# The end of a decode kernel: column tiles in two banks, projections ahead of V, and the last head woven into w4

## The chip, the cores and the metric

One NeuronCore of a Trainium2 chip runs the whole program. The time is that of one execution on the device, in microseconds (us), as the median over several runs. The profile is one execution taken by the hardware profiler; its times count from the start of its span. PE is TensorE, DVE is VectorE, ACT is ScalarE, POOL is GpSimd, and SP is SyncE, which here issues nearly all loads.

## The reference

Four tokens (B = 4, one position each, D = 576) go through a layer norm, and then through an attention block and an MLP block side by side, whose results are added:

```
xn = layernorm(x)
q  = xn @ wq                        # 32 heads of 128
k, v = the last 2048 positions of the caches, 16 heads, each used by 2 q heads
o  = softmax(q . k / sqrt(128)) @ v
A  = o @ wo                         # (4, 4096) @ (4096, 576)
h2 = gelu(layernorm(x1) @ w3) @ w4  # 576 -> 4608 -> 576
out = x + A + x1 + h2
```

With one position per token the shifts of the MLP's mixer move everything out of its single position, so that its first part adds zero and x1 is xn; w1 and w2 are not needed.

## The kernel before

The kernel is a stream of loads with work hung on it: wq, then 16 K tiles with w3 between the first of them, half of w4, 16 V tiles with eight tiles of wo between them, and the other half of w4. A K or V tile is one kv head of all four tokens, 2048 KB as 128 partitions x 64 chunks x 128. All of these loads are issued by SP, in the order of the program. SP waits with an issue until the buffer is free, and also until the load that stands eight issues back has landed; whatever is behind it on SP waits with it. The tiles of K, V, w3, w4 and the exponentials E share one pool of six buffers (`big`, NBUF, line 17), and wo has three of its own (line 87).

K is transposed on DVE (line 258), and scores of all heads add up in four banks S (line 267). `softmax` (from line 276) makes exponentials on ACT (line 283), normalizes them (lines 300 and 302), transposes the probabilities on PE (line 306) and puts them into PZ (lines 311 and 314).

The output of projection and MLP has 576 columns. PE computes them as two halves of DH = 288 columns, each on a 32-column tile of the array, with four rows (tokens) in use. So that four tiles work at the same time, the terms of the sums are shared between two pairs of tiles: in `acc_matmuls` (line 341) `half` picks the pair, and the result stands in partitions 64 x half + 32 x q. All four lie in one PSUM bank, ACC (line 182), which is zeroed once by a matmul (line 187). In its columns from 320 on, ACC also holds the MLP's first product. At the end the second pair is copied out (`second`, line 475) and added to the first (`fin`, line 481), and two small DMAs store the two halves of columns (line 483).

A row of w4 here is one of the 18 chunks into which each half of w4 is cut: 128 partitions x 576 elements, 147,456 bytes, two matmuls of 128x288. `load_w4(e, i0, n, cuts)` (line 420) takes one buffer for n rows of half e and fills it with one DMA for each number in `cuts`. `mlp_out` (line 431) does the matmuls of one piece, and its rows alternate between the two pairs of tiles, or use the first pair only where `last` is set. The first half is loaded whole ahead of V0 (line 452) and multiplied ahead of the softmax (line 457).

The V loop (line 461) stands under a manual schedule: PE's instructions keep the program's order there, while the other engines are ordered by the scheduler. For head v it issues V of head v + 4 and, for every second one, a tile of wo (lines 464 to 466). `v_compute(v)` (line 328) makes 16 matmuls into a bank O, four chunks at a time. `run_later` runs what the previous head left: for a pair of heads the projection (line 388, eight matmuls), and `select` of the head before (line 367). `head_out(v)` adds the four diagonal blocks of O into `osum` on DVE (lines 362 and 364). `select` lets PE sum and transpose osum (OT, line 370), DVE copy the result (`on`, line 372), PE spread it (line 375), and DVE write it to `onx` (line 383), the projection's stationary operand.

After the loop, half 1 of w4 is loaded in pieces of 9, 4, 2, 2 and 1 rows (line 470). PE multiplies the nine rows, runs the last head's select and the last projection, waits for `second`, and multiplies the last nine rows on the first pair alone (lines 471 to 477).

Of the kernel before, what the change touches and what calls it, by code (L numbers as in the profile page):

```python
# [12 lines left out]
F32 = mybir.dt.float32  # L13
# [7 lines left out]
def kernel(  # L21
# [18 lines left out]
    nc = tc.nc  # L40
    P = 128
    B, Sq, D = A_x.shape
    _, Hkv, Sk, Dh = A_k_cache.shape
    Hq = A_wq.shape[1] // Dh
    rep = Hq // Hkv
# [14 lines left out]
    NFH = NF // 2  # L60
    NQ = Hq * Dh
    DH = D // 2
# [26 lines left out]
    ps_s = ctx.enter_context(tc.tile_pool(name="ps_s", bufs=4, space=PSUM))  # L89
# [6 lines left out]
    def kv_load(win, h):  # L96
        t = big.tile([P, NCH, Dh], BF16, tag="big")
        nc.sync.dma_start(out=t[:].rearrange("p c d -> p (c d)"),
                          in_=win[:, h].rearrange("b (p c) d -> p b (c d)", p=G))
        return t  # L100
# [4 lines left out]
    XR = 4  # L105
# [24 lines left out]
    ident = const.tile([P, P], BF16)  # L130
# [27 lines left out]
    def transposed_pe(prep):  # L158
        src_bf, dup, T = prep
        tp = ps_tp.tile([P, KJ + 2, B], BF16, tag="tp")  # L160
        for j in range(KJ):
            nc.tensor.transpose(out=tp[:, j, :], in_=src_bf[:, j:KJ * P:KJ], identity=ident[0:B, 0:B])
        for e in range(2):
            nc.tensor.transpose(out=tp[:, KJ + e, :], in_=dup[:, e, :], identity=ident[0:B, 0:B])
        nc.vector.tensor_copy(out=T[:], in_=tp[:])

# [15 lines left out]
    ACC = ps_acc.tile([P, 512], F32)  # L182
    NR = 32 + B

    zeros = const.tile([P, 512], BF16)
    nc.vector.memset(zeros[:], 0.0)
    nc.tensor.matmul(out=ACC[:], lhsT=ident[:], rhs=zeros[:], start=True, stop=False, skip_group_check=True)
    GP0 = 320
    gp = ACC[:, GP0:GP0 + NF * B].rearrange("p (f b) -> p f b", b=B)
    gT = const.tile([P, NF, B], BF16)  # L190
# [35 lines left out]
    for y in range(NY):  # L226
        tq = ps_o.tile([P, 2 * HB, P], BF16, tag="O", name=f"tq{y}")
        for k in range(2):
            for m in range(HB):
                nc.tensor.transpose(out=tq[:, k * HB + m, :],  # L230
                                    in_=q_rows[:, k, m, y, :, :].rearrange("p g i -> p (g i)"), identity=ident[:])
# [18 lines left out]
    S = []  # L250
# [77 lines left out]
    def v_compute(h):  # L328
        bank = ps_o.tile([P, NI * Dh], F32, tag="O", name=f"O{h}")
        vn = V_tiles.pop(h)  # L330
        ns = NCH // (NI * NG)
        for s in range(ns):
            for j in range(NG):
                c0 = (s * NG + j) * NI
                nc.tensor.matmul(out=bank[G * j:G * j + G, :],  # L335
                                 lhsT=PZ[:, h, c0:c0 + NI, :].rearrange("p c m -> p (c m)"),
                                 rhs=vn[:, c0:c0 + NI, :].rearrange("p c d -> p (c d)"),
                                 start=(s == 0), stop=(s == ns - 1), skip_group_check=True)
        O_tiles[h] = bank

    def acc_matmuls(lhsT, rhs_cols, half):

        for q in range(2):
            o0 = 64 * half + 32 * q
            nc.tensor.matmul(out=ACC[o0:o0 + B, 0:DH], lhsT=lhsT, rhs=rhs_cols(q * DH, (q + 1) * DH),  # L345
                             start=False, stop=False, skip_group_check=True)

    wo_tiles = {}
# [2 lines left out]
    def load_wo(g2):  # L351
        wo_tiles[g2] = wop.tile([P, XR, D], BF16, tag="wo", name=f"wo{g2}")
        nc.sync.dma_start(out=wo_tiles[g2][:].rearrange("p x n -> p (x n)"), in_=wo_src[:, g2, :])

    later = []

    def head_out(h):


        bank = O_tiles.pop(h)  # L360
        osum = ktp.tile([P, Dh], F32, tag="kt", name=f"osum{h}")
        nc.vector.tensor_scalar_mul(out=osum[:], in0=bank[:, 0:Dh], scalar1=diag[:, 0:1])  # L362
        for i in range(1, NI):
            nc.vector.scalar_tensor_tensor(out=osum[:], in0=bank[:, i * Dh:(i + 1) * Dh], scalar=diag[:, i:i + 1],  # L364
                                           in1=osum[:], op0=ALU.mult, op1=ALU.add)

        def select():
            OT = ps_tp.tile([P, 64 + XR * rep * B], F32, tag="tp", name=f"OT{h}")
            T = OT[:, 64:64 + XR * rep * B].rearrange("p (x n) -> p x n", x=XR)
            nc.tensor.matmul(out=OT[:, 0:NB], lhsT=osum[:], rhs=sel[:], start=True, stop=True, skip_group_check=True)  # L370
            on = small.tile([P, rep, B], BF16, tag="on", name=f"on{h}")
            nc.vector.tensor_copy(out=on[:].rearrange("p r b -> p b r"),  # L372
                                  in_=OT[:, 0:NB].rearrange("p (b r) -> p b r", r=rep))
            for x in range(XR):
                nc.tensor.matmul(out=T[0:32, x, :], lhsT=ident[:, x:P:XR], rhs=on[:].rearrange("p r b -> p (r b)"),  # L375
                                 start=(x == 0), stop=(x == XR - 1), skip_group_check=True)
            g2, odd = divmod(h, 2)
            if not odd:
                onx_tiles[g2] = small.tile([P, XR, B], BF16, tag="onx", name=f"onx{g2}")
            onx = onx_tiles[g2]  # L380
            for r in range(rep):
                q = 32 * (2 * odd + r)
                nc.vector.tensor_copy(out=onx[q:q + 32, :, :], in_=T[0:32, :, r * B:(r + 1) * B])  # L383
            if odd:
                wt = wo_tiles.pop(g2)
                onx_tiles.pop(g2)

                def project():
                    for x in range(XR):
                        acc_matmuls(onx[:, x, :], lambda a, z, x=x: wt[:, x, a:z], x % 2)  # L390
                later.append(project)
        later.append(select)

    def run_later():
        fns = later[:]
        later.clear()
        for fn in fns:
            fn()

    def g_piece(t, j):  # L400
        for fc in range(NF):
# [18 lines left out]
    def load_w4(e, i0, n, cuts):  # L420
        t = big.tile([P, n, D], BF16, tag="big", name=f"w4_{e}_{i0}")
        parts = []
        a = 0
        for m in cuts:
            nc.sync.dma_start(out=t[:, a:a + m, :], in_=w4_src[e, :, i0 + a:i0 + a + m, :])
            parts.append((t[:, a:a + m, :], e, i0 + a, m))
            a += m
        assert a == n
        return parts

    def mlp_out(t, e, i0, n, last=False):
        for i in range(n):
            acc_matmuls(gT[:, e * NFH + i0 + i, :], lambda a, z, i=i: t[:, i, a:z], 0 if last else i % 2)


    for h in range(Hkv):
# [12 lines left out]


    NV0 = 4
    w4 = load_w4(0, 0, NFH, (NFH,))
    for v in range(NV0):
        V_tiles[v] = kv_load(v_win, v)
    for g2 in range(2):
        load_wo(g2)
    mlp_out(*w4[0])
    PZ = softmax()

    with tc.manual_schedule(engines={mybir.EngineType.PE}):  # L460
        for v in range(Hkv):
            n = v + NV0
            if n < Hkv:
                V_tiles[n] = kv_load(v_win, n)
                if n % 2 == 0:
                    load_wo(n // 2)
            v_compute(v)
            run_later()
            head_out(v)
        end = load_w4(1, 0, 9, (9,)) + load_w4(1, 9, 9, (4, 2, 2, 1))  # L470
        mlp_out(*end[0])
        while later:
            run_later()
        second = const.tile([P, DH], F32)
        nc.vector.tensor_copy(out=second[0:NR, :], in_=ACC[64:64 + NR, 0:DH])  # L475
        for part in end[1:]:
            mlp_out(*part, last=True)
    assert not K_tiles and not V_tiles and not wo_tiles

    fin = const.tile([P, DH], out.dtype)  # L480
# [33 lines left out]
```

## Time and profile before

| what | value |
|---|---|
| median of 3 runs | 216.41 us (216.26 to 216.51) |
| the profiled execution, its own time | 216.26 us |
| its span | 214.5 us |
| HBM read | 87.17 MB, 406 GB/s over the span |
| DVE busy | 130.2 us (61%) |
| PE busy | 112.2 us (52%), mean granted clock 0.676 |
| ACT busy | 21.0 us (10%) |

The span ends 1.76 us short of the time of that execution, since what lies around the span is not in it. A row of a group names the line, the engine, the operation, and then out<-in with the tiles' names; "x16" is a count. In the table of windows, each stretch has the busy time of each engine with the number of instructions, then the granted clock of TensorE (1.00 is full speed), the mean busy share of the 16 DMA engines and the rate at which they moved data. Ends of matmuls are modelled, so that a duration of one matmul is longer than the distance between two of them.

### The profile page before, as it was taken

To read this page: it belongs to the slowest core of one execution; us is meant where nothing else is said; L and a number is where in the kernel's file an instruction comes from. 1 tells how busy PE (TensorE), PEld (TensorE's weight loads), DVE (VectorE), ACT (ScalarE), POOL (GpSimd) and SP (SyncE) were. 2 spreads that over 40 slices of the span, in tenths; PEclk is the share of its full clock that TensorE was granted. 3 is DMA by queue.
4 is the path that set the end of the run, shared out by engine and by line. 5 is a ranking of instruction groups with operands and counts; after the bars stand their busy time and mean duration, and the time that the engine had idled before them with its cause. 6 is when DMAs were issued, how large, how long until landed. Compare 5 with 4: busy or idle time off the path is not lost.

```text
span 214.5 us, 4125 instructions
## 1 busy us (share of the span) xinstructions
PE 112.2 (52%) x1841; PEld 57.1 (27%) x1841; DVE 130.2 (61%) x223; ACT 21.0 (10%) x36; POOL 1.8 (1%) x8
## 2 busy tenths in 40 slices
PE   0383797774345544454442195735555554646374
PEld 0123484741111111111101162423232221313141
DVE  7949525369999999899675691862424142324241
ACT  0204100000000000000004896000000000000000
POOL 1110000000000000000000000000000000000000
PEclk9999995558579758665578569995555555555555
DMA  6999999999999999999999999999999999999940
GB/s 251 434 440 422 440 439 408 440 425 426 422 440 422 428 434 434 425 425 425 443 431 419 434 428 421 432 443 407 437 420 434 432 442 410 435 428 430 411 191 1
DMA packets 7529, 87.43 MB, mean 408 GB/s; under 512 B 844, under 2 KB 984, under 8 KB 2648
## 3 DMA queue, kind: packets, MB, share of 16 engines
q1 hardware_dynamic: 7496, 87.17, 95.8%
q8 instruction: 14, 0.23, 0.4%
q10 hardware_dynamic: 16, 0.01, 0.0%
q14 instruction: 3, 0.02, 0.0%
HBM read 87.17 MB, written 0.00 MB: 406 GB/s over the span
## 4 chain that ended last, share of the span: by engine, by line
DMA 66%; DVE 15%; PE 11%; ACT 5%; issue 2%; SPq 1%; DVEq 0%
DMA t<-in_A_v_cache_dram 38%; DMA t<-in_A_k_cache_dram 22%; DVE kt L258 10%; DMA wq<-in_A_wq_dram 6%; PE O L335 4%; PE ACC L345 3%; PE pt L306 2%; ACT E L283 2%; ACT PZ L311 1%; ACT pr L300 1%; DVE q_rows L224 1%; DVE pr L302 1%; PE qp L208 1%; PE OT L370 1%; DVE osum L362 0%
## 5 line engine op out<-in xcount | busy, mean ns | idle before, releaser
L258 DVE STREAM_TRANSPOSE kt<-t 128x2048 int32<-128x2048 int32 x32 | 72.0, 2290 | 15.4 <-DMA t<-in_A_k_cache_dram 15.4
L267 PE MATMUL S<-kt,qz 32*32 32x512 bf16 x1024 | 37.3, 625 | 40.2 <-DVE kt L258 37.8
L335 PE MATMUL O<-t,PZ 128*32 128x512 bf16 x256 | 27.9, 550 | 29.3 <-DMA t<-in_A_v_cache_dram 27.6
L362 DVE TENSOR_SCALAR osum<-O,diag 128x128 f32<-128x128 f32 x16 | 5.6, 350 | 39.8 <-PE O L335 39.8
L267 PEld LDWEIGHTS <-qz 32*32 32x32 bf16 x1024 | 10.6, 94 | 63.5 <-issue 59.9
L335 PEld LDWEIGHTS <-PZ 128*32 128x32 bf16 x256 | 9.2, 118 | 37.6 <-issue 33.9
L364 DVE SCALAR_TENSOR_TENSOR osum<-O,diag,osum 128x128 f32<-128x128 f32 x48 | 16.6, 348 | 1.0
L306 PE MATMUL pt<-ident,pr 128*128 128x128 bf16 x64 | 5.8, 265 | 9.2 <-DVE pr L302 8.2
L283 ACT ACTIVATE E<-S,nb 128x512 f32<-128x512 f32 x4 | 4.0, 1114 | 62.6 <-DMA t<-in_A_v_cache_dram 62.6
L370 PEld LDWEIGHTS OT<-sel,osum 128*128 128x128 f32 x32 | 7.2, 281 | 10.8 <-issue 5.2
L407 PEld LDWEIGHTS <-w 128*128 128x128 bf16 x144 | 9.1, 163 | 1.6 <-DMA w<-in_B_w_dram 0.8
L370 PE MATMUL OT<-sel,osum 128*128 128x8 f32 x32 | 8.6, 343 | 1.5 <-DVE osum L364 1.5
L407 PE MATMUL ACC<-ln2T,w 128*128 128x4 bf16 x144 | 9.3, 202 | 0.0
L300 ACT ACTIVATE pr<-E,rdm 128x512 bf16<-128x512 f32 x6 | 8.0, 1419 | 0.7 <-DVE rdm L289 0.7
L306 PEld LDWEIGHTS <-pr 128*128 128x128 bf16 x64 | 5.0, 121 | 10.5 <-ACT pr L300 10.3
L302 DVE TENSOR_SCALAR pr<-E,rdm 128x512 bf16<-128x512 f32 x10 | 6.4, 793 | 0.3 <-PE pt L306 0.2
L383 DVE CAST onx<-OT 32x16 bf16<-32x16 f32 x32 | 5.3, 165 | 2.0 <-PE OT L375 0.4
L375 PE MATMUL OT<-on,ident 128*32 128x8 bf16 x64 | 4.2, 171 | 4.1 <-DVE on L372 4.1
L345 PE MATMUL ACC<-wo,onx 128*4 128x288 bf16 x64 | 5.5, 424 | 0.4 <-DVE onx L383 0.4
L345 PE MATMUL ACC<-w,gT 128*4 128x288 bf16 x72 | 5.1, 366 | 0.9 <-DVE second L475 0.6
L375 PEld LDWEIGHTS <-ident 128*32 128x32 bf16 x64 | 4.5, 110 | 4.0 <-issue 3.6
L230 PE MATMUL tq<-ident,q_rows 128*128 128x128 bf16 x32 | 3.8, 312 | 2.7 <-ACT q_rows L222 2.7
(74 smaller groups left out, 62.9 us busy)
## 6 DMA issues: line engine op xcount, KB each, us to landing
t<-in_A_k_cache_dram SPq DMA_DIRECT2D x16, 2048.0 KB, 23.5
t<-in_A_v_cache_dram SPq DMA_DIRECT2D x16, 2048.0 KB, 21.8
w<-in_B_w_dram SPq DMA_DIRECT2D x2, 2304.0 KB, 24.9
wo<-in_A_wo_dram SPq DMA_DIRECT2D x8, 576.0 KB, 20.7
wq<-in_A_wq_dram SPq DMA_DIRECT2D x2, 2048.0 KB, 10.1
w<-in_B_w_dram SPq DMA_DIRECT2D x1, 2592.0 KB, 27.2
w<-in_B_w_dram SPq DMA_DIRECT2D x1, 1296.0 KB
w_t<-in_B_w_dram SPq DMA_DIRECT2D x1, 576.0 KB, 26.3
```

What stands on the lines that cost most here:

```text
L258: nc.vector.transpose(out=ap32(kt, e * G * 2, [[2 * G * 2, NCH // 2], [1, 2], [2, G]]), in_=ap32(kn, e * G, [[2 * 2 * G, NCH // 2], [2 * G ...
L267: nc.tensor.matmul(out=S[g][32 * b:32 * b + 32, :].rearrange("p (c k l) -> p c k l", k=GK, l=2), lhsT=qz[32 * g:32 * g + 32, b, h, y, :], ...
L283: nc.scalar.activation(out=E[:, :, g, :].rearrange("p (c l) k -> p c k l", l=2), in_=S[g][:].rearrange("p (c k l) -> p c k l", k=GK, l=2), ...
L300: nc.scalar.mul(out=dst, in_=src, mul=rdm[:, b:b + 1])
L302: nc.vector.tensor_scalar_mul(out=dst, in0=src, scalar1=rdm[:, b:b + 1])
L306: nc.tensor.transpose(out=tp[:, cc, :], in_=pr[:, half * HC + cc, :, :, :].rearrange("p g k b -> p (g k b)"), identity=ident[:])
L335: nc.tensor.matmul(out=bank[G * j:G * j + G, :], lhsT=PZ[:, h, c0:c0 + NI, :].rearrange("p c m -> p (c m)"), rhs=vn[:, c0:c0 + NI, :].rear ...
L345: nc.tensor.matmul(out=ACC[o0:o0 + B, 0:DH], lhsT=lhsT, rhs=rhs_cols(q * DH, (q + 1) * DH), start=False, stop=False, skip_group_check=True)
L364: nc.vector.scalar_tensor_tensor(out=osum[:], in0=bank[:, i * Dh:(i + 1) * Dh], scalar=diag[:, i:i + 1], in1=osum[:], op0=ALU.mult, op1=AL ...
L370: nc.tensor.matmul(out=OT[:, 0:NB], lhsT=osum[:], rhs=sel[:], start=True, stop=True, skip_group_check=True)
L375: nc.tensor.matmul(out=T[0:32, x, :], lhsT=ident[:, x:P:XR], rhs=on[:].rearrange("p r b -> p (r b)"), start=(x == 0), stop=(x == XR - 1), ...
L407: nc.tensor.matmul(out=gp[:, fc, :], lhsT=lhsT, rhs=rhs, start=False, stop=False, skip_group_check=True)
```

## The change

The second pair of column tiles gets a bank of its own: `ACC2`, a buffer of the pool `ps_s` (the one of S), zeroed by a matmul at the start of the manual schedule; `acc_matmuls` writes `ACCS[half]`. Until then only the first pair is used. The list `later` is split: projections run ahead of the next head's `v_compute`, selects stay behind it, and `select` is cut into `transpose_sum` (OT and `on`) and the rest. Of the first half of w4 only nine rows are loaded ahead of V0; the other nine come after V15, in front of half 1. So 27 rows are loaded at the end, in pieces of 9, 5, 4, 5, 3 and 1, and the steps of the last head stand between the pieces. `mlp_out`'s argument `last` is now called `one`.

```diff
@@ -185,6 +185,7 @@
     nc.tensor.matmul(out=ACC[:], lhsT=ident[:], rhs=zeros[:], start=True, stop=False, skip_group_check=True)
+    ACCS = [ACC]
@@ -340,9 +341,10 @@
     def acc_matmuls(lhsT, rhs_cols, half):
         for q in range(2):
             o0 = 64 * half + 32 * q
-            nc.tensor.matmul(out=ACC[o0:o0 + B, 0:DH], lhsT=lhsT, rhs=rhs_cols(q * DH, (q + 1) * DH),
+            nc.tensor.matmul(out=ACCS[half][o0:o0 + B, 0:DH], lhsT=lhsT, rhs=rhs_cols(q * DH, (q + 1) * DH),
                              start=False, stop=False, skip_group_check=True)
@@ -352,7 +354,7 @@
-    later = []
+    selects, projects = [], []
@@ -364,13 +366,16 @@
-        def select():
+        def transpose_sum():
             OT = ps_tp.tile([P, 64 + XR * rep * B], F32, tag="tp", name=f"OT{h}")
-            T = OT[:, 64:64 + XR * rep * B].rearrange("p (x n) -> p x n", x=XR)
             nc.tensor.matmul(out=OT[:, 0:NB], lhsT=osum[:], rhs=sel[:], start=True, stop=True, skip_group_check=True)
             on = small.tile([P, rep, B], BF16, tag="on", name=f"on{h}")
             nc.vector.tensor_copy(out=on[:].rearrange("p r b -> p b r"),
                                   in_=OT[:, 0:NB].rearrange("p (b r) -> p b r", r=rep))
+            return OT, on
+
+        def select(OT, on):
+            T = OT[:, 64:64 + XR * rep * B].rearrange("p (x n) -> p x n", x=XR)
@@ -388,14 +393,12 @@
-                later.append(project)
-        later.append(select)
-
-    def run_later():
-        fns = later[:]
-        later.clear()
-        for fn in fns:
-            fn()
+                projects.append(project)
+        selects.append((transpose_sum, select))
+
+    def run_projects():
+        while projects:
+            projects.pop(0)()
@@ -449,32 +452,43 @@
     NV0 = 4
-    w4 = load_w4(0, 0, NFH, (NFH,))
+    w4 = load_w4(0, 0, 9, (9,))
     for v in range(NV0):
         V_tiles[v] = kv_load(v_win, v)
     for g2 in range(2):
         load_wo(g2)
-    mlp_out(*w4[0])
+    mlp_out(*w4[0], one=True)
     PZ = softmax()
 
     with tc.manual_schedule(engines={mybir.EngineType.PE}):
+        ACC2 = ps_s.tile([P, 512], F32, tag="S", name="ACC2")
+        nc.tensor.matmul(out=ACC2[:], lhsT=ident[:], rhs=zeros[:], start=True, stop=False, skip_group_check=True)
+        ACCS.append(ACC2)
         for v in range(Hkv):
             n = v + NV0
             if n < Hkv:
                 V_tiles[n] = kv_load(v_win, n)
                 if n % 2 == 0:
                     load_wo(n // 2)
+            run_projects()
             v_compute(v)
-            run_later()
+            if selects:
+                tsum, select = selects.pop()
+                select(*tsum())
             head_out(v)
-        end = load_w4(1, 0, 9, (9,)) + load_w4(1, 9, 9, (4, 2, 2, 1))
+        end = load_w4(0, 9, 9, (9,)) + load_w4(1, 0, 9, (5, 4)) + load_w4(1, 9, 9, (5, 3, 1))
+        tsum, select = selects.pop()
         mlp_out(*end[0])
-        while later:
-            run_later()
+        last = tsum()
+        mlp_out(*end[1])
+        select(*last)
+        mlp_out(*end[2])
+        run_projects()
+        mlp_out(*end[3])
         second = const.tile([P, DH], F32)
-        nc.vector.tensor_copy(out=second[0:NR, :], in_=ACC[64:64 + NR, 0:DH])
-        for part in end[1:]:
-            mlp_out(*part, last=True)
+        nc.vector.tensor_copy(out=second[0:NR, :], in_=ACC2[64:64 + NR, 0:DH])
+        for part in end[4:]:
+            mlp_out(*part, one=True)
```

More of the change, by code (lines that the diff above doesn't have):

```diff
@@ L429, in load_w4, with mlp_out @@
         return parts
-    def mlp_out(t, e, i0, n, last=False):
+    def mlp_out(t, e, i0, n, one=False):
         for i in range(n):
-            acc_matmuls(gT[:, e * NFH + i0 + i, :], lambda a, z, i=i: t[:, i, a:z], 0 if last else i % 2)
+            acc_matmuls(gT[:, e * NFH + i0 + i, :], lambda a, z, i=i: t[:, i, a:z], 0 if one else i % 2)
     for h in range(Hkv):
```

## The prediction

> **What bounds the kernel now.** The page's slices over time come first.
>
> ```profile
> PE   0383797774345544454442195735555554646374
> ...
> PEclk9999995558579758665578569995555555555555
> DMA  6999999999999999999999999999999999999940
> GB/s 251 434 440 422 440 439 408 440 425 426 422 440 422 428 434 434 425 425 425 443 431 419 434 428 421 432 443 407 437 420 434 432 442 410 435 428 430 411 191 1
> ```
>
> A slice is 5.36 us. The DMA row is full from the second slice to the 38th (203.8 us), so up to there the time is bytes over rate and no engine matters. The changed kernel loads the same 87.17 MB. The last two slices are different: little or nothing is loaded, and 10.7 us pass. They are read from the chain that ended last, in order of time (start, duration, what):
>
> ```profile
> 182.62 19.38 DMA t<-in_A_v_cache_dram
> 202.00 0.04 issue
> 202.04 1.90 PE O L335 x12
> 203.94 0.48 PE ACC L345 x6
> 204.42 0.54 PE OT L370 x2
> ...
> 206.68 0.54 PE OT L370 x2
> ...
> 208.16 0.68 PE ACC L345 x8
> 208.84 0.02 issue
> 208.87 0.47 DVE second L475
> 209.34 0.04 issue
> 209.38 2.34 PE ACC L345 x18
> 211.72 0.02 issue
> 211.74 0.45 DVE fin L481
> ```
>
> The last V lands at 202.00. After it come V's products, head 14's select, nine rows of w4, head 15's select and projection, the copy `second`, nine more rows, `fin`. When did the data for those last nine rows land? The windows show where loading stops (stretch, busy times, clock, DMA share, GB/s), and the answer on line 425 gives issue and landing.
>
> ```profile
> 204.50:205.00 0.50, 0.44 (x2) 0.45 (x3) 0.24 (x2) 0.00 (x0) 0.00 (x0) 0.50 0.88 339
> ...
> 207.50:208.00 0.50, 0.23 (x4) 0.14 (x3) 0.22 (x2) 0.00 (x0) 0.00 (x0) 0.50 0.26 90
> 208.00:208.50 0.50, 0.34 (x8) 0.23 (x9) 0.11 (x1) 0.00 (x0) 0.00 (x0) 0.50 0.00 0
> ```
> ```profile
> L425 SPq DMA_DIRECT2D w<-in_B_w_dram x6: 327/334/592, 85.8 to 190.9; - x6
> ...
> DMA to landing us min/median/max: 17.4/22.2/27.2
> ```
>
> The last piece was issued at 190.85 and took 17.4 (the minimum, that of the 144 KB piece): it landed at 208.25, and nothing moves after 208.0. So between landing and `fin` lie 211.74 - 208.25 = 3.49 us in which TensorE works off a backlog: nine rows waited for the copy, the copy for the projection, the projection for the chain of head 15. That is what the change can take.
>
> **The pace of the stream.** From V15's landing (202.00) to the end (208.25), 18 rows of 147,456 bytes came: 6.25 / 18 = 0.347 us a row, 425 GB/s. I use it for the new order.
>
> **The pieces of the change.**
>
> *Nine rows of w4 move from ahead of V0 to behind V15.* Nothing is added to the stream. 27 rows now follow V15, so it lands at 208.25 - 27 x 0.347 = 198.88, and the pieces at 202.00 (9), 203.74 (5), 205.13 (4), 206.86 (5), 207.90 (3), 208.25 (1). What covers the move: V5's issue waits until the exponentials are used up (SP issues it at 131.19). Before, the queue still held work then: after the first w4 landed (113.06) came five V tiles and three wo, 12.26 MB, 28.6 us at 428 GB/s, so it emptied at 141.7. Now it empties 9 x 0.347 = 3.1 earlier, at 138.6, which leaves 7.4 us. Cost 0; without that cover, each us of dry queue would be a us. The other issues on SP keep their order. wo3 and the next V behind it went at 139.45 and 139.84 with V5 and V6 (4.9 us each) hardly begun. Their wait is for a projection, which the change puts earlier (ahead of V, not behind). The last piece's issue has to wait for the landing of the tile eight issues back, V14 now (192.6, from 195.7 less 3.1): 15.6 us ahead of its need. Cost 0.
>
> *First piece of w4, 18 matmuls on two column tiles instead of 36 on four.* V4's issue waits for them (114.44). Two tiles took 2.34 us for 18 (the last row of the chain), the 36 took 1.33 here: at most +1.0, with over 15 us of queue. Cost 0.
>
> *The bank ACC2 and its zeroing.* The nearest row for one 128x512 matmul of zeros is 0.59 (line 187). It stands ahead of V0's products, and in the order of the new program all 64 transposes of the probabilities now stand ahead of it, where V0's products were mixed in before. Behind it wait V0's products, whose end frees V6's buffer. Between 0 and +1.5 us there, under the 7.4 us: cost 0.
>
> *Projection ahead of the next V.* PE sat idle for V every time (1.4 to 3.4 us), so its 0.72 fits there. For pair 6 it removes 0.5 to 0.7 between V15's products and head 14's select.
>
> *The woven end, on PE and VectorE, from rows of the same instructions.* V14 (no projection behind it) gives distances from the first product: OT matmul +1.83, select matmuls +2.68, last osum done +4.10. So, from 198.92: OT 200.75, select 201.60, rows free at 201.9, osum15 done 203.02. Nine rows start at 202.04 (landing). Before, nine rows from 205.23 let the next OT start at 206.61: 1.38, or 0.153 a row. So:
> - 202.04 nine rows; 203.42 OT of head 15 (0.60; osum has been done 0.4); `on` done 204.22
> - 204.02 five rows (0.77); 204.79 select; `onx` ready 0.70 later (207.46 to 208.16 before), 205.49
> - 205.17 four rows (0.61); 205.78 projection (0.65); 206.43 PE is free
> - 206.90 five rows (landing), 0.77 and 0.2 until the last ends: 207.87. `second` (0.47) reads ACC2 until 208.4, beside the next rows, as ACC is no longer the same bank
> - 207.94 three rows and, from 208.25 on, the last: four rows on two tiles at 2.34 / 9 = 0.26 are 1.04: 208.98
> - `fin` starts at 209.01 instead of 211.74
>
> From `fin` to the end nothing changes. The sum is -2.73 us. The profiled execution took 216.26 (span 214.5 and 1.76 around it), which is the lowest of the three runs (median 216.41): 213.5 us.
>
> **Costs without a row, and their ends.**
> - End of stream: earlier if the pieces' new sizes let the 16 engines finish together. Their idle share between 204.5 and 208.0 adds up to 1.6 us. The 27 rows take 9.37 us; at the slowest 4 us window since 142 (398 GB/s) they would take 0.64 more, at the fastest (455) 0.62 less. I take 0, since engines and bytes are the same, and keep -0.6 and +0.64 in the range; the 1.6 stays outside as unlikely.
> - A row on four tiles in two banks: 0.13 (two rows' pairs abreast at 0.26) to 0.52 (one matmul after the other, twice 0.26). I take 0.153, the same four tiles in one bank.
> - OT followed directly by rows is not in the trace: 0 to 0.45 (one row matmul's duration), against 0.46 us in which PE waits for the fifth piece. 0. The Trainium skill speaks against it: "TensorEngine Tiling (Array Packing)", Key Properties, says that a change of tiling mode, not just of tile, drains TensorE. The woven order adds such changes, and no row here shows one alone; by that rule the sum would lose those few tenths of slack and stay as it is.
> - The granted clock: 0.50 in all windows from 146 us on, also from 202 to 207, where PE was busy 4.7 of 5 us. PE will now be busy for 9 of 10 us. At full clock, which the trace grants from 128 to 142, the last four rows would take half: -0.5. I take 0.50, the row from the same place, and keep -0.5. The Trainium skill ("TensorE: Matmul & The Clock Gate", What's actually happening) says that about 3.4 us of sustained activity in a free-running window lifts the throttle; by that the sum would be 213.0, but the 4.9 us here did not lift it.
>
> **Rivals.**
> 1. *PE is late.* The steps above leave PE 0.1 to 0.46 us of slack each. If drains and waits of the woven order cost 1 us more than that, the end follows: 214.5. For: PE's work after V15 is about 9 us beside 9.4 of stream. Against: all terms are start-to-start distances of this trace, with their waits in them. Chance 0.13.
> 2. *Two banks cost the overlap*, the one that ends slower. If matmuls to different banks did not run abreast, a row would cost 0.52. PE's work from 202.04 is 1.9 us of fixed steps and 27 rows or their like (23 rows, the projection's four), so `fin` is late against 211.74 from 0.29 a row on; at 0.52 it starts at 218.0, 222.5 in all. Against: the 32 scores' matmuls that write four banks take 1.13 us, 35 ns each, while one lasts 625 ns on average. Chance 0.04.
> 3. *The queue runs dry at V5* by more than 2.7 us, which needs 10 us of delay: 0.02, ends same or slower.
> 4. *It does not do what it says*: the copy or the chain still waits behind the last load. In the new order of PE the chain stands between the pieces, and `second` waits for ACC2's last matmul only, so 0.02, 216.3.
>
> **Numbers.** The forecast has 0.79: 213.5, its bounds 212.4 (clock and fast stream, -1.1) to 214.2 (slow stream). With rival 1 and some of its drains the range is 212.4 to 214.8. This kernel's measurement can tell about 0.2% from no change. Faster: forecast and rival 1, 0.92; same 0.03; slower 0.05.
>
> **What will show it.** In the new trace: V15's products near 198.9; DMA share zero from about 208.0; OT of head 15 ahead of 204; `second` beside row matmuls; one to two rows' work between the last landing and `fin`, near 209. I am wrong if the last landing moves by over 0.6, if PE has no wait for the fifth and sixth piece, or if V's landings after V5 show a gap.

## The result, and the profile after

The changed kernel takes 213.76 us (median of 4 runs, 213.76 to 213.90) against 216.41 (216.26 to 216.51): 0.988 of the time before, with a 95% interval of 0.9863 to 0.9897. The profiled execution took 213.90, with a span of 212.1, so 1.8 lie around the span, as before. The forecast was 213.5, in a range of 212.4 to 214.8.

First come two rows of the slices over time on the page of the changed kernel: the busy share of the DMA engines in tenths, and their rate. A slice is 5.30 us now.

```profile
DMA  6999999999999999999999999999999999999980
GB/s 248 442 430 441 414 426 440 420 430 431 423 430 436 414 430 436 439 417 433 417 436 426 439 424 438 412 441 417 439 414 434 435 424 436 422 430 431 415 347 35
```

Loads fill the time as they did, to the 38th slice, and the HBM read is the same 87.17 MB. What has become shorter is the stretch without loads at the end. The chain that ended last (start, duration, what) of the changed kernel shows it:

```profile
188.02 20.13 DMA w<-in_B_w_dram
...
208.19 1.14 PE ACC L347 x8
...
209.35 0.45 DVE fin L495
```

Behind the last loads stands one group of eight matmuls, and then `fin`. Before, the end of this chain had V's products, two selects, a projection, the copy and 18 matmuls. The end of the loads themselves is where it was, to a quarter of a us: the last piece landed at 208.5, and before at 208.25. Here is a window of the changed kernel (stretch, busy times, clock, DMA share, GB/s), after which nothing is loaded:

```profile
208.00:208.50 0.50, 0.33 (x6) 0.21 (x5) 0.30 (x1) 0.00 (x0) 0.00 (x0) 0.50 0.04 12
```

And PE's instructions in order of time at the end, from V15's products on (start, duration, line, tiles, count, and in brackets the idle time ahead of it with what ended it):

```profile
199.16 1.90 PE L336 MATMUL O<-t,PZ 128*32 128x512 bf16 x16 [2.22 <-DMA t<-in_A_v_cache_dram]
...
202.23 1.36 PE L347 MATMUL ACC<-w,gT 128*4 128x288 bf16 x18
203.52 0.60 PE L371 MATMUL OT<-sel,osum 128*128 128x8 f32 x2
204.05 0.88 PE L347 MATMUL ACC<-w,gT 128*4 128x288 bf16 x10
...
205.40 0.65 PE L347 MATMUL ACC<-w,gT 128*4 128x288 bf16 x8 [0.39 <-DMA w<-in_B_w_dram]
205.83 0.70 PE L347 MATMUL ACC<-wo,onx 128*4 128x288 bf16 x8
207.14 0.88 PE L347 MATMUL ACC<-w,gT 128*4 128x288 bf16 x10 [0.61 <-DMA w<-in_B_w_dram]
208.19 1.12 PE L347 MATMUL ACC<-w,gT 128*4 128x288 bf16 x8 [0.17 <-DMA w<-in_B_w_dram]
```

On DVE, the copy that used to stand between the projection and the last rows:

```profile
207.84 0.46 DVE L489 COPY second<-ACC 36x288 f32<-36x288 f32 x1 [2.44 <-PE ACC L347]
```

It ends at 208.30, and the last rows no longer wait for it: they began at 208.19. Read the brackets: at 205.40, 207.14 and 208.19 PE waits for loads. PE has no backlog any more; it is the loads that it waits for until 208.15, when the piece of three lands. Then the last four rows follow: these three, and the one of the last piece.

`fin` starts at 209.35 instead of 211.74, 2.39 us earlier; the two profiled executions differ by 216.26 - 213.90 = 2.36, the medians by 2.65. (The profiled execution before was the fastest of its runs, the one after the slowest.)

### The profile page after: what moved, and what is told of

Same layout as the page of the kernel before. It is cut to its first block, busy times and chain, and to the rows that moved or that the text cites. A ratio compares the mean times of both kernels' runs of the same rounds, so it can differ in the third digit from the quotient of the medians.

```text
span 212.1 us, 4131 instructions
## 1 busy us (share of the span) xinstructions
PE 118.4 (56%) x1842; PEld 58.9 (28%) x1842; DVE 130.4 (61%) x223; ACT 21.0 (10%) x36; POOL 1.8 (1%) x8
## 3 DMA queue, kind: packets, MB, share of 16 engines
q1 hardware_dynamic: 7640, 87.17, 96.9%
HBM read 87.17 MB, written 0.00 MB: 411 GB/s over the span
## 4 chain that ended last, share of the span: by engine, by line
DMA 69%; DVE 14%; PE 9%; ACT 4%; SPq 1%; issue 1%; DVEq 0%; ACTq 0%
DMA t<-in_A_k_cache_dram 35%; DMA t<-in_A_v_cache_dram 19%; DMA w<-in_B_w_dram 9%; DVE kt L259 9%; DMA wq<-in_A_wq_dram 6%; PE O L336 3%; PE pt L307 3%; ACT E L284 2%; ACT pr L301 1%; DVE q_rows L225 1%; PE ACC L347 1%; DVE mx L280 1%; DVE pr L303 1%; ACT PZ L312 1%; PE qp L209 1%
## 5 line engine op out<-in xcount | busy, mean ns | idle before, releaser
L336 PE MATMUL O<-t,PZ 128*32 128x512 bf16 x256 | 29.6, 612 | 16.6 <-DMA t<-in_A_v_cache_dram 16.6
L336 PEld LDWEIGHTS <-PZ 128*32 128x32 bf16 x256 | 9.8, 131 | 27.5 <-issue 26.5
L307 PE MATMUL pt<-ident,pr 128*128 128x128 bf16 x64 | 7.4, 311 | 11.4 <-DVE pr L303 8.3
L307 PEld LDWEIGHTS <-pr 128*128 128x128 bf16 x64 | 6.5, 145 | 12.4 <-ACT pr L301 12.4
L371 PE MATMUL OT<-sel,osum 128*128 128x8 f32 x32 | 9.1, 358 | 0.8 <-DVE osum L366 0.8
L347 PE MATMUL ACC<-w,gT 128*4 128x288 bf16 x72 | 6.5, 408 | 1.3 <-DMA w<-in_B_w_dram 1.2
```

What stands on the lines that cost most here:

```text
L307: nc.tensor.transpose(out=tp[:, cc, :], in_=pr[:, half * HC + cc, :, :, :].rearrange("p g k b -> p (g k b)"), identity=ident[:])
L336: nc.tensor.matmul(out=bank[G * j:G * j + G, :], lhsT=PZ[:, h, c0:c0 + NI, :].rearrange("p c m -> p (c m)"), rhs=vn[:, c0:c0 + NI, :].rear ...
L347: nc.tensor.matmul(out=ACCS[half][o0:o0 + B, 0:DH], lhsT=lhsT, rhs=rhs_cols(q * DH, (q + 1) * DH), start=False, stop=False, skip_group_che ...
```

## The experiments

Theory A is the prediction's: the loads end where they did, and the gain is what PE no longer has to do after the last landing. Theory B is a rival: projections and the loads of wo and V behind them are issued earlier, and so the stream itself is faster. All ratios are to the kernel before, run again beside each group of these on the same chip. Its median was 216.44 to 216.47 there and 216.41 with the result, so that medians of different groups can be set side by side to about 0.1. Single runs stray further: of 35 of the kernel before, two took 215.13 and 215.39, and one of e3's four took 213.28.

| run | median us (range) | ratio, 95% interval |
|---|---|---|
| e1_bank_only | 215.66 (215.57 to 215.85) | 0.997, 0.9957 to 0.9983 |
| e4_weave_only | 214.45 (214.34 to 214.56) | 0.9913, 0.9895 to 0.9931 |
| e5_move_only | 213.91 (213.76 to 214.09) | 0.9888, 0.987 to 0.9906 |
| e2_one_bank | 214.23 (214.07 to 214.34) | 0.9903, 0.9885 to 0.992 |
| e3_proj_behind | 213.82 (213.28 to 213.96) | 0.9869, 0.9855 to 0.9884 |
| e6_small_last | 213.64 (213.46 to 213.71) | 0.9868, 0.9855 to 0.9881 |
| e7_all_behind | 214.90 (214.24 to 215.29) | 0.9923, 0.9909 to 0.9938 |
| e8_zero_behind | 213.80 (213.74 to 213.87) | 0.9877, 0.9864 to 0.9889 |
| e9_all_and_zero_behind | 214.05 (213.66 to 214.41) | 0.9889, 0.9873 to 0.9904 |
| e10_small_last_zero_behind | 213.50 (213.42 to 213.59) | 0.9864, 0.9847 to 0.988 |

**The second bank alone.** In the kernel before:

```diff
+    ACCS = [ACC]
...
-            nc.tensor.matmul(out=ACC[o0:o0 + B, 0:DH], lhsT=lhsT, rhs=rhs_cols(q * DH, (q + 1) * DH),
+            nc.tensor.matmul(out=ACCS[half][o0:o0 + B, 0:DH], lhsT=lhsT, rhs=rhs_cols(q * DH, (q + 1) * DH),
...
-    mlp_out(*w4[0])
+    mlp_out(*w4[0], last=True)
...
+        ACC2 = ps_s.tile([P, 512], F32, tag="S", name="ACC2")
+        nc.tensor.matmul(out=ACC2[:], lhsT=ident[:], rhs=zeros[:], start=True, stop=False, skip_group_check=True)
+        ACCS.append(ACC2)
...
-        nc.vector.tensor_copy(out=second[0:NR, :], in_=ACC[64:64 + NR, 0:DH])
+        nc.vector.tensor_copy(out=second[0:NR, :], in_=ACC2[64:64 + NR, 0:DH])
```

> The kernel before with the second bank alone; w4's 18 rows ahead of V0 all go to the first pair of tiles. Theory A (the time after the last landing is PE's backlog): the last 18 matmuls no longer wait for the copy, which cost 0.56 us of idle PE; they follow the projection at 208.8 and take 2.33, fin near 211.1: 0.6 us less, 215.7 to 215.9. Theory B (the gain came from the stream, since projections and so wo and V issues are earlier): nothing in the stream moves, and the copy was in cover: 216.3.

215.66. PE and DVE at the end of this run, in order of time:

```profile
208.67 2.37 PE L346 MATMUL ACC<-w,gT 128*4 128x288 bf16 x18
208.94 0.46 DVE L479 COPY second<-ACC 36x288 f32<-36x288 f32 x1 [0.75 <-PE ACC L346]
211.08 0.45 DVE L485 TENSOR_TENSOR fin<-ACC,second 36x288 bf16<-36x288 f32 x1 [1.68 <-PE ACC L346]
```

The copy at 208.94 lies beside the 18 matmuls, which began 0.27 us ahead of it, right behind the projection (208.24); before, they waited until 209.38. `fin` at 211.08, as theory A had it (211.1). Theory B gave no change.

**The weave without the move.** In the changed kernel:

```diff
-    w4 = load_w4(0, 0, 9, (9,))
+    w4 = load_w4(0, 0, NFH, (NFH,))
-        end = load_w4(0, 9, 9, (9,)) + load_w4(1, 0, 9, (5, 4)) + load_w4(1, 9, 9, (5, 3, 1))
+        end = load_w4(1, 0, 9, (5, 4)) + load_w4(1, 9, 9, (5, 3, 1))
...
-        mlp_out(*end[3])
-        for part in end[4:]:
+        for part in end[3:]:
```

> The changed kernel with 18 rows of w4 ahead of V0 as before, so 18 rows behind V15 in pieces of 5, 4, 5, 3 and 1 with the last head woven in. Theory A: V15 lands at 202.0 again, osum of head 15 is done 4.1 us after the first product (206.15), and the chain from there sets the end: OT 206.2, four rows, select 207.4, five rows, projection 208.5 to 209.1, four rows on two tiles until 210.2. Fin 210.2 against 211.74: 214.7. Theory B: all of the gain, 213.8, as the issues are as early as in the changed kernel.

214.45. It keeps the issue order that theory B relies on and yet is 0.69 slower than the changed kernel. Its PE at the end:

```profile
206.37 0.57 PE L371 MATMUL OT<-sel,osum 128*128 128x8 f32 x2 [0.55 <-DVE osum L366]
...
208.54 1.24 PE L347 MATMUL ACC<-w,gT 128*4 128x288 bf16 x8
```

Here PE waits for DVE (osum of head 15), not for a load: V15 lands 3 us later, and the chain from it sets the end. `fin` came at 209.83, 0.4 before my 210.2: I let groups of matmuls follow one another from end to end, while the next group starts 0.2 to 0.3 before the end that the profile shows (the projection took 0.78 from 208.05 on, so until 208.83, and the next rows began at 208.54).

**The move without the weave.** In the changed kernel, the last head's steps in one piece:

```diff
         mlp_out(*end[0])
-        last = tsum()
+        select(*tsum())
+        run_projects()
         mlp_out(*end[1])
-        select(*last)
         mlp_out(*end[2])
-        run_projects()
         mlp_out(*end[3])
```

> The changed kernel with 27 rows behind V15, but the last head's steps in one piece behind the first nine rows. Theory A: PE idles through the chain's waits (about 1.3 us), the projection ends at 205.8, nine rows that have landed take until 207.1, and the piece of five lands at 207.1: PE is in time, and the time is the changed kernel's, 213.8. Rival (the weaving is what brings the gain): the waits push everything back by 1 us, 214.7.

213.91, within 0.15 of the changed kernel, whose runs it overlaps. Its PE at the end:

```profile
205.73 1.41 PE L347 MATMUL ACC<-w,gT 128*4 128x288 bf16 x18
207.33 0.88 PE L347 MATMUL ACC<-w,gT 128*4 128x288 bf16 x10 [0.19 <-DMA w<-in_B_w_dram]
```

PE does idle through the chain's waits (0.44 us for `onx` ahead of the projection is one), and nine rows have piled up by 205.73. They are done 0.19 before the next piece lands. So with 27 rows behind V15 and two banks the weave is not needed; the move is what brings the time down, and the weave brings most of it only where the rows are not moved (e4).

**One bank.** In the changed kernel:

```diff
-        ACC2 = ps_s.tile([P, 512], F32, tag="S", name="ACC2")
-        nc.tensor.matmul(out=ACC2[:], lhsT=ident[:], rhs=zeros[:], start=True, stop=False, skip_group_check=True)
-        ACCS.append(ACC2)
+        ACCS.append(ACC)
...
-        nc.vector.tensor_copy(out=second[0:NR, :], in_=ACC2[64:64 + NR, 0:DH])
+        nc.vector.tensor_copy(out=second[0:NR, :], in_=ACC[64:64 + NR, 0:DH])
```

> The changed kernel with one bank for both pairs. Theory A: the last four rows have to wait for the copy (207.84 to 208.30 in the changed kernel) and start near 208.36 instead of 208.19: 0.17 us more, 213.9 to 214.0. Rival (two banks change the pace of the rows): a change of more than 0.5 us in the rows between 202 and 208, and 213.3 or 214.4.

214.23, 0.2 to 0.3 above what I gave theory A. The end of its chain:

```profile
207.96 0.47 DVE second L487
208.43 0.04 issue
208.47 1.14 PE ACC L347 x8
```

The copy has become a link of the chain, as expected. It starts later than I thought: 0.92 us after the first matmul of the piece of five (207.04), where the changed kernel's copy started 0.70 after (207.14 and 207.84). That it now waits for the last matmul on either pair, and not for the last on its own, would explain this; no run separates it. The pace of rows is the same as in two banks: the 18 matmuls of nine rows took 1.36 us in both kernels, from the first to the next OT 1.29.

**Projections behind V's products, as before.**

```diff
-            run_projects()
             v_compute(v)
+            run_projects()
```

> The changed kernel with the projections behind the next head's products, as before. Theory A: wo is issued later by one V tile, but the queue of loads always has work; behind V15 the projection of pair 6 delays head 14's select by 0.5 us and the nine rows by 0.3, and PE still waits for the piece of four: 213.8. Theory B (earlier issues make the stream faster): the last landing moves back, 214.3 or more.

213.82, with the last pieces at the same times (its rows of the piece of five began at 207.18, of three at 208.26). Theory B falls: this edit has no effect that these runs can tell.

**Smaller last pieces.**

```diff
-        end = load_w4(0, 9, 9, (9,)) + load_w4(1, 0, 9, (5, 4)) + load_w4(1, 9, 9, (5, 3, 1))
+        end = load_w4(0, 9, 9, (9,)) + load_w4(1, 0, 9, (5, 4)) + load_w4(1, 9, 9, (5, 2, 1, 1))
```

> The changed kernel with the last nine rows in pieces of 5, 2, 1 and 1 instead of 5, 3 and 1. Theory A: the end is set by the landing of the piece of three (208.15), behind which eight matmuls stand (1.12). With 2, 1, 1 landing at 207.8, 208.15 and 208.5, two rows are done by 208.45, and one pair is left after the last landing, or two: fin at 209.0 to 209.1 instead of 209.35, 213.4 to 213.5. Rival (small pieces cost the stream as much): 213.8 or more.

213.64, between the two. The profiled execution was the fastest of its four (213.46). In order of time:

```profile
206.98 1.87 PE L347 MATMUL ACC<-w,gT 128*4 128x288 bf16 x18 [0.59 <-DMA w<-in_B_w_dram]
...
208.89 0.45 DVE L495 TENSOR_TENSOR fin<-ACC,second 36x288 bf16<-36x288 f32 x1 [0.76 <-PE ACC L347]
```

The last nine rows now run without a gap from the landing of the piece of five: 1.91 us from there to `fin`, where the changed kernel took 209.35 - 207.14 = 2.21. That is the 0.3 forecast, in the profile; of the medians' 0.12 alone I would not say that it is a gain.

**All 36 rows behind V15.**

```diff
-    w4 = load_w4(0, 0, 9, (9,))
-    mlp_out(*w4[0], one=True)
+        w0 = load_w4(0, 0, 9, (9,))
         end = load_w4(0, 9, 9, (9,)) + load_w4(1, 0, 9, (5, 4)) + load_w4(1, 9, 9, (5, 3, 1))
         tsum, select = selects.pop()
+        mlp_out(*w0[0])
         mlp_out(*end[0])
```

> The changed kernel with no w4 ahead of V0, so that 36 rows follow V15 (nine more ahead of the woven part). Theory A: the stream has the same bytes, and the queue at V5 still has 4.3 us of work when V5 is issued: the last landing and the time stay, 213.8. Rival (the cover at V5 is thinner than worked out): a gap in the loads between 131 and 145 us, and 0.5 us or more on the time.

214.90: 1.1 slower than the changed kernel. Theory A is wrong here, in its figure for the cover. Windows of this run, first the stretch between V5 and V6, then the 20 us around it:

```profile
138.00:139.00 1.00, 0.74 (x18) 0.68 (x21) 0.70 (x4) 0.00 (x0) 0.00 (x0) 1.00 0.57 197
130.00:150.00 20.00, 16.16 (x154) 8.12 (x155) 9.22 (x34) 2.08 (x2) 0.00 (x0) 0.59 0.98 388
```

The changed kernel in the same two:

```profile
138.00:139.00 1.00, 0.74 (x14) 0.67 (x18) 0.68 (x4) 0.00 (x0) 0.00 (x0) 1.00 1.11 475
130.00:150.00 20.00, 16.05 (x154) 7.99 (x154) 9.13 (x33) 2.20 (x2) 0.00 (x0) 0.59 1.02 431
```

43 GB/s less over 20 us is 0.86 MB, 2.0 us of stream; about 1 us of that reached the end (`fin` at 210.36 instead of 209.35). My sum had 4.3 us of work left in the queue at V5's issue.

The trace also records each load's completions, 16 to a load, and a load has landed with the last of them. Those of wo2, the last load in the queue ahead of V5, came from 132.15 to 135.24 in this run, so that the landing is 3.1 us behind the first. V5 was issued at 131.10, only 1.05 us ahead of that first one. Its own first completion came 5.90 us behind wo2's first, where a tile takes 4.85 (135.35 to 140.20 in the changed kernel); V6's came 5.73 behind V5's (143.78 and 138.05). So the DMA engines that were ahead ran dry twice, and it shows up to the end: the last piece's completions came from 207.51 to 209.52, where the changed kernel had 205.24 to 208.50. The first lost 2.3 us, the last 1.0.

**The zeroing behind V0's products.** In the changed kernel the three lines of ACC2 stand behind `v_compute(0)`:

```diff
-        ACC2 = ps_s.tile([P, 512], F32, tag="S", name="ACC2")
-        nc.tensor.matmul(out=ACC2[:], lhsT=ident[:], rhs=zeros[:], start=True, stop=False, skip_group_check=True)
-        ACCS.append(ACC2)
...
             v_compute(v)
+            if v == 0:
+                ACC2 = ps_s.tile([P, 512], F32, tag="S", name="ACC2")
+                nc.tensor.matmul(out=ACC2[:], lhsT=ident[:], rhs=zeros[:], start=True, stop=False, skip_group_check=True)
+                ACCS.append(ACC2)
```

> The changed kernel with ACC2 zeroed behind V0's products instead of ahead of them; V0's products are then mixed between the transposes of the probabilities again. In the changed kernel the granted clock was 0.50 from 125 to 135 us, where it was 0.78 to 1.00 before, V6 was issued 1.6 us later and wo3 2.3 us later. Theory A: the clock comes back to 1.00 from about 128, the issues come earlier again, and the time stays at 213.8, as the queue of loads covered it. Rival (the slower clock cost part of the gain): 213.3 or less.

213.80. The window from 130 to 135 us, first of the changed kernel, then of this run; the column ahead of the DMA share is the granted clock:

```profile
130.00:135.00 5.00, 3.75 (x33) 2.35 (x37) 0.69 (x1) 2.20 (x2) 0.00 (x0) 0.50 1.00 424
```
```profile
130.00:135.00 5.00, 3.32 (x39) 1.61 (x39) 1.60 (x4) 2.32 (x2) 0.00 (x0) 1.00 1.02 430
```

The clock came back, SP's pair of issues (V5 and V6) took 3.17 again instead of 4.76, wo3 went at 139.80 instead of 141.71, and the time stayed.

**The edits of e7 and e8 together.**

The diffs are those of e7 and e8.

> No w4 ahead of V0 (36 rows behind V15), and ACC2 zeroed behind V0's products, so that V6 and the next wo are issued 1.6 and 2 us earlier than in the run with all rows behind alone, which took 214.9 and showed a dip of the loads at 138 to 139 us. Theory C (the queue of the fast DMA engines ran dry between V5 and V6, some 4 us before the landings say so): with V6 issued at 133.8 the dip goes or shrinks, the last landing comes back by most of its 1 us, 213.8 to 214.3. Rival (the order of the bytes at the end, 36 rows of w4 in a row, is what costs): no change, 214.9.

214.05, 0.85 below e7. Its profiled execution was its slowest (214.41), and still moved more in the 20 us than e7 (403 GB/s against 388). The stretch from 138 to 139 us is not below what the changed kernel has in one of these 20 us (328 GB/s from 143 to 144):

```profile
130.00:150.00 20.00, 15.79 (x156) 7.74 (x158) 10.15 (x37) 2.10 (x2) 0.00 (x0) 0.67 0.98 403
138.00:139.00 1.00, 0.57 (x7) 0.38 (x3) 0.70 (x3) 0.00 (x0) 0.00 (x0) 1.00 0.77 328
```

V6 was issued at 133.96 here, 1.35 us ahead of e7's 135.31. Its first completion came 4.86 us behind V5's (142.97 and 138.11), a tile's usual time, so that the second dry stretch is gone; the first one, at V5, stays (5.92 from wo2's first completion to V5's).

So the late issue of V6 made most of e7's loss, and not the order of bytes at the end, which is the same in both: an edit that was worth nothing in e8 was worth 0.85 here. The other 0.3 to the changed kernel stay, with the dry stretch at V5. The ranges of e7 and e9 touch (214.24 to 215.29, 213.66 to 214.41), so that the size is rough; the completions are those of one execution of each.

**Small last pieces with the zeroing behind.**

The diffs are those of e6 and e8.

> The changed kernel with the last pieces 5, 2, 1 and 1 and ACC2 zeroed behind V0's products. If what is left after the last landing is one pair of matmuls, fin and the store, and nothing but the stream stands before it, the second edit adds nothing to the first: 213.4 to 213.7, as with small pieces alone. If the later issues of V6 and wo3 cost the stream a few tenths (the last V landed 0.24 later than forecast), 213.2 to 213.3.

213.50; all its runs (213.42 to 213.59) lie below all of the changed kernel's (213.76 to 213.90), though they were measured on another occasion. The profiled end is that of e6 (rows from 206.98, `fin` at 208.89). It beats both kernels, by 0.26 us over the changed one, and as far as these runs tell, the small pieces do it: e10 and e6 lie within 0.14 of each other.

## Why the prediction was right

- *What bounds it, and the backlog of 3.49 us.* Right: `fin` came 3.49 after the last landing before. Now it comes about 0.9 after (the piece of one row was issued at 192.88 and took 15.6, so it landed at 208.48), where the sum had 0.76.
- *The pace and the landings.* 0.347 us a row held: V15 to the piece of three is 26 rows, and took 208.15 - 199.12 = 9.03, 0.347 each. But all of it stands 0.24 later than I put it (199.12 against 198.88; the piece of five 207.10 against 206.86). This is the larger part of the miss of 0.34 in `fin`. e6, e3 and e5, with the same stream to that point, had the piece of five at 206.94, 207.14 and 207.29, so that the place of the stream scatters by some 0.3 from run to run; all are later than I said. Why is open: the edits of e3 and e8 do not move it beyond that scatter. In the time the miss is smaller for another reason: the sum was taken off the profiled 216.26, the fastest run before. Off the median, 216.41 - 2.73 = 213.68, against 213.76 measured.
- *Moved rows and projections: cost 0.* Right in the time, but the cover of 7.4 us was counted from landings and is thinner. In the changed kernel wo2's completions came from 135.35 to 138.54 and V5 was issued at 131.22: 7.3 us to the last, as forecast, but 4.1 to the first. In e7, 1.05 us to the first were about 1.05 too few (5.90 against 4.85), so that V5's data took about 2 us from the issue to flow. That leaves some 2 of the 7.4 us: an estimate from one execution of each. The term was harmless at this size, and mis-sized; that the 3.1 us of the move fitted was closer than the sum said.
- *The zeroing: 0 to +1.5 us ahead of V6's issue.* It was +1.6 (from 133.8 to 135.4), just outside. With V0's products behind all transposes, the zeroing (at 132.93) and then all 16 products of V0 (from 133.49) had to run there, at half clock. e8 takes away all of this at once, so that the zeroing's share and the clock's are not separated. Hidden, as said.
- *The woven end.* Each step within 0.25, most of that the landings: head 15's OT at 203.52 (203.42), rows 204.05 (204.02), select 204.72 (204.79), projection 205.83 (205.78). The last four rows took 1.16 to `fin` instead of 1.07. What the sum did not say is that the weave was not needed for it: e5 has the time without it.
- *Costs without a row.* A row in two banks: 1.29 / 9 = 0.143 (0.153 taken), so rival 2 is out. The drain: rows follow OT after 0.53, where the sum took 0.60. So the drain at a change of tiling mode that I cited from the Trainium skill ("TensorEngine Tiling (Array Packing)", Key Properties) added nothing to the sum; whether one lies hidden in the 0.53, no run here shows. Rival 1 is out, since PE waits for the pieces of four, five and three rows (0.39, 0.61 and 0.17). The clock stayed at 0.50 to the end.
- *Chances.* The forecast's case held: copy beside rows, waits for the fifth and sixth piece (five and three rows). The sign in the prediction to look for, a gap after V5, is absent at this size and present in e7.

The parts do not add up: bank 0.8, bank and weave 2.0, bank and move 2.6, move and weave 2.2, all 2.65 (differences of medians from 216.47 and 216.41). Each takes from the same 3.49 us, and once the loads are waited for, further cuts on PE ahead of the last landings are worth nothing.

## What to carry to other kernels

Where loads fill the time, look at what is left to do after the last landing, load last what has the shortest tail (here weights with one pair of matmuls a row, not V with a chain of 10 us), and try smaller last pieces (0.1 to 0.3 us here, near the scatter). Cover that is counted from landings is thinner than it seems: a load's landing is its last completion, 3.1 to 3.4 us behind its first here, and the engines that are done first run dry first. An edit that costs nothing today can cost time after another edit has used up the same cover.

## What the runs showed of the hardware

The granted clock does not follow PE's busy share. A window at the end of the changed kernel, where PE was busy 4.62 of 5 us (the first busy time) at a clock of 0.50:

```profile
200.00:205.00 5.00, 4.62 (x52) 2.55 (x45) 1.97 (x8) 0.00 (x0) 0.00 (x0) 0.50 1.00 411
```

In the kernel before, PE was busy 0.96 of 2 us at a clock of 1.00:

```profile
128.00:130.00 2.00, 0.96 (x11) 0.19 (x4) 0.79 (x2) 2.00 (x3) 0.00 (x0) 1.00 0.96 408
```

"TensorE: Matmul & The Clock Gate" of the Trainium skill (What's actually happening) has the throttle lifted by about 3.4 us of sustained activity, in a window that runs freely. The traces agree with the window: the granted clock is 1.00 or 0.50 in them and changes at multiples of 3.41 us. They do not agree with busy time as the measure. Here are two pairs of such windows of the changed kernel, the first among the scores of K, the second at the end:

```profile
86.17:89.58 3.41, 1.89 (x64) 0.48 (x43) 3.29 (x2) 0.00 (x0) 0.00 (x0) 0.50 1.04 447
89.59:93.00 3.41, 1.33 (x48) 0.31 (x32) 3.05 (x2) 0.00 (x0) 0.00 (x0) 1.00 0.98 418
...
202.23:205.64 3.41, 3.02 (x42) 1.75 (x45) 1.44 (x7) 0.00 (x0) 0.00 (x0) 0.50 0.93 381
205.64:209.05 3.41, 2.63 (x34) 1.07 (x26) 0.46 (x1) 0.00 (x0) 0.00 (x0) 0.50 0.31 122
```

A window with 1.89 us of scores was followed by full clock, one with 3.02 us of row matmuls was not. Matmuls with four stationary columns may count for less; no run here separates that.

Nor does a short gap decide. Ahead of V0's products PE stood for 0.66 us at 126.1 to 126.9 both in the changed kernel and in e7. The 16 transposes behind it took 1.89 us in the one and 1.07, the time at full clock, in the other, and the window with the gap was busy for 0.81 of its time in both. What made the difference, no run shows. In e7 the clock was lost again at 130.2, within an idle stretch of 3.28 us.

The 16 completions of a load lie 3.1 to 3.4 us apart in the changed kernel from 128 us on, and still at the last piece (205.24 to 208.50). In the kernel before, the mean share of the DMA engines falls from 0.88 to 0.26 from 204.5 to 208.0, which is the same spread seen at the end. This is what I left out of the cover at V5. Running dry cost more than the idle time: over the 20 us of e7 the share fell by 4% (1.02 to 0.98) and the rate by 10%. In the record of single transfers, some of 16 KB took up to 1.47 us from 137.5 to 139.5 us there, where none took over 0.61 in the changed kernel. Why is open.
